# Two attentions on one core: Q and K by halves in two units, and a new order around the first unit's exponentials

## The chip, the cores and the metric

The kernel runs on one core of a Trainium2 chip. The metric is device time in microseconds (us), from the first to the last instruction with the little that lies around it; lower is better.

## What is computed

Two attention layers, independent of each other, with inputs of 2048 positions by 1024 features, 32 heads of 32 features, all in float32. Layer A is dilated: each position attends to 8 positions, two apart. Layer B is a sliding window of 256 positions. Both project the input to Q, K and V, and project the result with `wo`.

```python
qkv = (x @ wqkv).reshape(B, S, 3, H, Dh).transpose(2, 0, 3, 1, 4)
# layer A: W, dil = 8, 2; idx = pos[:, None] - arange(W) * dil, masked where negative
logits = einsum("bhsd,bhswd->bhsw", q, kg) * Dh ** -0.5
o = einsum("bhsw,bhswd->bhsd", softmax(logits), vg)
# layer B: mask = (i - j >= 0) & (i - j < 256)
scores = einsum("bhqd,bhkd->bhqk", q, k) * Dh ** -0.5
o = einsum("bhqk,bhkd->bhqd", softmax(where(mask, scores, -1e9)), v)
# both
return o.transpose(0, 2, 1, 3).reshape(B, S, D) @ wo
```

## The kernel before

**Units and head groups.** The work is cut into eight units of 512 positions: units 0 to 3 are layer B, units 4 to 7 layer A. In the code `u` is the unit, `DU` is 4 (the units of layer B), `U` is 8, and `s` counts the eight head groups (`NG`) of four heads in a unit; `hg = u * NG + s` numbers them through. Layer A's second and third unit are thus units 5 and 6, layer B's first is unit 0. All matmuls are done in three terms on values that are split in a high and a low part, so each x group and each weight is split after loading: a cast on ScalarE or VectorE (L276 or L279), then a subtraction on VectorE (L282). Loads go through three `raw` buffers; a buffer is loaded again when its split is done.

**Projections.** For each head group, Q and K are one accumulation each over eight blocks (`NK`) of three matmuls, the k-th block reading the k-th eighth of x and of the weights. x comes in four groups of two eighths. The list of items to load has, in units 5 and 6, Q's weights, x groups 0 and 1, K's weights, x groups 2 and 3. At the end of the unit before, the last part of V (narrow: two banks, sixteen blocks) is mixed with four items that ask for the next unit's x groups, one every four blocks from the second place on; asking writes the group's split into the engines' order.

**PSUM.** Three banks (`rg`) serve projections, four (`rs`) scores, one (`ro`) the values' results. Each ring gives out its banks in turn. A bank can be taken again when the copy that empties it is done: for V `copy_out` (L720 when on ScalarE), for Q and K `evac` (L625 in layer B, L586 and L591 in layer A).

**Attention of layer B.** `first` makes 16 score tiles for a head group. For each, `top` on VectorE (L1398) masks and takes the maximum, `total` on ScalarE (L1403) takes exponentials and their sum, which frees the score bank. When all 16 are done, `log_sum` and `parts` make the logarithm of the sums, `rows` puts it with a small matmul against the identity into rows, and `spread` (L1438) writes these into Q's stacked tile. Then `second` makes the scores anew, transposed, with the sums taken off; their exponentials (L1483) are masked, and `values` multiplies them with V. Q and K reach their stacked tiles by copies that SP issues, for units with a predecessor the last 256 keys of the unit before as well (`read_halo`). Layer A's scores work on small tiles (`window`).

**The order.** A planner in the Python code sets the order of every engine's instructions. It keeps a clock per engine with fixed costs, and four lists: row transpositions, second scores and values, first scores, and projections. At each step it takes the item that can start first by these clocks. Work that follows on other engines is written into their order when its time comes in the plan (`ck.defer(t, f)`: not before `t`). On the chip each engine runs its instructions in the order so written, waiting for semaphores. `done["stack"]` is the time from which the plan takes a head group's keys as there: the last copy's landing and `KEYS_LATE`, 1.2 us; `aux` holds the row transpositions.

Of the kernel before, what the change touches and what calls it, by code (L numbers as in the profile page):

```python
# [15 lines left out]
NG = 8  # L16
NK = 8
# [274 lines left out]
def kernel(ctx, tc, xs, wqk, wv, wo, outs, units):  # L292
# [271 lines left out]
    def latest(*ts):  # L564
        return None if any(t is None for t in ts) else max(ts)


    def qk_items(u, s):
# [8 lines left out]
        def read_halo():  # L577
            hb = halo[(u + 1) % 2][s]
            for r, a in enumerate((0, 1, 0)):
                nc.sync.dma_start(kst[buf][r:96:3, :, :256].bitcast(F32), hb[:, a])  # L580
                ck.copy("halo_in", ck.now)

        def evac_window(t, ps, bank):
            if t == 0:
# [35 lines left out]
        def evac(t, ps, bank):  # L620
            if not dense:
                return evac_window(t, ps, bank)
            hl = natp.tile([P, 2 * S + 16], F32R, tag="nat", name="nat")[:, :2 * S].rearrange("p (a s) -> p a s", a=2)
            sc = SCALE if t == 0 else 1.0
            nc.scalar.activation(hl[:, 0, :], ps, AF.Copy, scale=sc)  # L625
            r = ck.use("act", 0.485, ck.now + ck.SEM)

            def low():
                nc.vector.scalar_tensor_tensor(hl[:, 1, :], ps, sc, hl[:, 0, :].bitcast(F32), op0=ALU.mult,
                                               op1=ALU.subtract)  # L630
                e = ck.use("dve", 0.61, r)
                rg.give(bank, e)

                def stack():
                    e2 = place(1, e)
                    if t == 1:
                        done["stack"][u, s] = max(e2, h2["hi"]) + KEYS_LATE
                    if t == 1 and u + 1 < U and units[u + 1][3]:
                        nc.sync.dma_start(halo[u % 2][s], hl[:, :, 256:].bitcast(F32))
                        e2 = ck.copy("halo_out", e, ck.now)  # L640
                    done["nat"][2 * hg + t] = max(e2, h2["hi"])

                later(stack)

            def place(part, e):
                dst, c = (qst[buf], 0) if t == 0 else (kst[buf], 256)
                for i, a in enumerate((0, 0, 1) if t == 0 else (0, 1, 0)):
                    if a == part:
                        nc.sync.dma_start(dst[i:96:3, :, c:c + S].bitcast(F32), hl[:, a, :].bitcast(F32))
                        e2 = ck.copy("copy", e, ck.now)  # L650
                return e2

            def stack_hi():
                if t == 0 and has_halo:
                    read_halo()
                h2["hi"] = place(0, r)

            def later(f):
                if hg < 2 or hg - 2 in done["second"]:
                    f()  # L660
                else:
                    waiting.setdefault(hg - 2, []).append(f)

            later(stack_hi)
            ck.defer(r, low)
# [704 lines left out]
    def attention(u, s):  # L1370
# [11 lines left out]
        def first(b, j):  # L1382
            if "nm" not in h:
                h["nm"] = small.tile([P, 16], F32, tag="nm", name="nm")
                h["sm"] = small.tile([P, 16], F32, tag="sm", name="sm")
            full, mask = 384, cst["mask_d"]
            cut = 0 if has_halo else max(0, 256 - P * b)
            n = full - cut
            c1 = 256 + P * b + P
            c0 = c1 - n  # L1390
            i = j * 4 + b
            ps, bank = rs.take()
            mm(ps[:, :n], q[0:96, j, b * P:(b + 1) * P], kk[0:96, j, c0:c1],
                             start=True, stop=True)
            nm, sm = h["nm"][:, i:i + 1], h["sm"][:, i:i + 1]

            def top():
                nc.vector.tensor_tensor_reduce(ps[:, :n], ps[:, :n], mask[:, cut:full], scale=-1.0, scalar=BIG,  # L1398
                                               op0=ALU.add, op1=ALU.min, accum_out=nm)
                e = ck.use("dve", n / 960 + 0.114, ck.now) + 0.06  # L1400

                def total():
                    nc.scalar.activation(ps[:, :n], ps[:, :n], AF.Exp, bias=nm, scale=-1.0, accum_out=sm)  # L1403
                    e2 = ck.use("act", n / 1200 + 0.236, e)
                    rs.give(bank, e2)
                    h["left"] -= 1
                    if h["left"] == 0:
                        ck.defer(e2, log_sum)

                ck.defer(e - 0.1, total)  # L1410

            return top

        def log_sum():
            ln = small.tile([P, 16], F32, tag="ln", name="ln")
            nc.scalar.activation(ln, h["sm"], AF.Ln)
            e = ck.use("act", 0.13, ck.now) - 0.03

            def parts():
                nl = small.tile([P, 16], F32, tag="nl", name="nl")  # L1420
                nc.vector.tensor_tensor(nl, h["nm"], ln, op=ALU.subtract)
                hl = small.tile([P, 2, 16], F32R, tag="hl", name="hl")
                nc.vector.tensor_copy(hl[:, 0, :], nl)
                nc.vector.tensor_tensor(hl[:, 1, :], nl, hl[:, 0, :].bitcast(F32), op=ALU.subtract)
                e2 = ck.use("dve", 0.52, e, port=True)
                aux.append(Item(lambda: latest(rs.when(BANK_LATE), e2), lambda: rows(hl), 0.08))

            ck.defer(e, parts)

        def rows(hl):  # L1430
            ps, bank = rs.take()
            mm(ps[0:32, 0:P], hl.rearrange("p a b -> p (a b)"), cst["ident"], start=True, stop=True)

            def spread():

                h["rows"] = []
                for j in range(4):
                    nc.vector.tensor_tensor(q[96:P, j, :].rearrange("p (b s) -> p b s", s=P),  # L1438
                                            ps[0:32, None, 0:P].to_broadcast([32, 4, P]),
                                            cst["pick"][0:32, 4 * j:4 * j + 4, None].to_broadcast([32, 4, P]), op=ALU.mult)  # L1440
                    e = ck.use("dve", 0.61, ck.now)
                    h["rows"].append(e + ROWS_LATE)
                rs.give(bank, e)

            return spread
# [124 lines left out]
    for p in plan:  # L1570
        if not marks and p[1:] == (DU, 2) and p[0] == "qk":
            marks.append(len(gemm))
        if len(marks) == 1 and p[0] == "p":
            marks.append(len(gemm))
        if p[0] == "qk":
            new = qk_items(p[1], p[2])
            if p == ("qk", 0, 0):
                q, k, x = new[:NK], new[NK:], x_items(0)
                f = dict(FILL)
                new = x[0] + sum([q[i:i + 1] + fill(i + 1, f.get(i + 1, 0)) for i in range(4)], [])  # L1580
                for i in (1, 2, 3):
                    new[new.index(q[2 * i]) if i < 2 else len(new):0] = x[i]
                    if i == 1:
                        new += k[:4]
                    else:
                        new += q[2 * i:2 * i + 2] + k[2 * i:2 * i + 2]
            if p[1:] == (0, NG - 1):
                x1 = x1 or x_items(1)
                for g in range(3, FIRST_X - 1, -1):
                    new[NK + 2 * g - 2:NK + 2 * g - 2] = x1[g]  # L1590
            gemm += new
        elif p[0] == "v":
            new = v_items(p[1], p[2])
            if p[1:] == (0, 2) and FIRST_X:
                x1 = x_items(1)
                for g in range(FIRST_X - 1, -1, -1):
                    new[X1_AT[g]:X1_AT[g]] = x1[g]
            elif V_SLOTS.get(NG - 1) == p[2] and 0 < p[1] < U - 1:
                m = 2 * VPARTS[p[2]][1]
                for g, x in reversed(list(enumerate(x_items(p[1] + 1)))):  # L1600
                    new[m * g + XAT:m * g + XAT] = x
            gemm += new
        elif p[0] == "o":
            gemm += o_items(p[1], p[2])
        elif p[0] == "p":
            gemm += product(p[1], p[2])
        elif p[0] == "vp":
            new = value_product(p[2])
            if VP_AT.get((p[1], NG - 1)) == p[2:] and p[1] + 1 < U:
                for g, x in reversed(list(enumerate(x_items(p[1] + 1)))):  # L1610
                    new[4 * g + XAT:4 * g + XAT] = x
            gemm += new
# [87 lines left out]
```

## Time and profile before

| what | value |
|---|---|
| median of 3 runs | 1789.3 us (1788.56 to 1789.42) |
| the profiled execution | 1788.09 us, span 1786.4 us |
| TensorE (PE) busy | 1768.4 us, 99% of the span |
| VectorE (DVE) busy | 1295.5 us, 73% |
| ScalarE (ACT) busy | 936.9 us, 52% |
| GpSimd (POOL) busy | 412.8 us, 23% |
| HBM | 201.33 MB read, 53.48 MB written |

A row of the timeline has the start in us, the duration, the engine, the line, the operation, its tiles as out<-in, shapes and the count of instructions merged in it; in brackets the engine's idle time before it and what ended it. The stages' rows have, for each stretch, its length and each engine's busy time. Tile `g` is a projection's bank, `s` a score bank, `o` the values' bank; with `g`, the tile named first after the arrow is the one that streams.

### The profile page before, as it was taken

What the parts mean: (1) busy time and instruction counts of PE and PEld (TensorE: products, weight loads), DVE (VectorE), ACT (ScalarE), POOL (GpSimd) and SP (SyncE); (2) the same over time, 40 slices, a digit from 0 to 9 for tenths busy, and PEclk for the clock granted to TensorE, in tenths of its full rate; (3) what the DMA queues carried; (4) which work ended last, traced back from release to release, by engine and by line L of the source; (5) the groups of instructions that cost most, each with busy time, mean ns of one, the idle gap of its engine ahead of it and who ended that gap; (6) DMA issues with size and microseconds to landing.
All of it is one profiled execution on the core that took longest, in us unless ns stands there. A gap on an engine that the chain in (4) does not pass through costs nothing.

```text
span 1786.4 us, 38443 instructions
## 1 busy us (share of the span) xinstructions
PE 1768.4 (99%) x14496; PEld 1440.2 (81%) x14496; DVE 1295.5 (73%) x2881; ACT 936.9 (52%) x2332; POOL 412.8 (23%) x962
## 2 busy tenths in 40 slices
PE   9999999999999999999999999999999999999999
PEld 7787778888777888778788788878888887877887
DVE  6777876768867769867669546566577868767866
ACT  5565566555656565655654524444354546455442
POOL 3322324222333233242323410110011101001210
PEclk9999999999999999999999999999999999999999
DMA  8354664645645556555556255656576758948984
GB/s 256 106 151 136 187 167 137 163 135 152 186 142 154 154 127 173 150 148 156 133 142 186 72 181 180 210 193 209 175 219 197 233 169 290 303 151 271 310 319 144
DMA packets 154793, 324.57 MB, mean 182 GB/s; under 512 B 18032, under 2 KB 58992, under 8 KB 154608
## 3 DMA queue, kind: packets, MB, share of 16 engines
q0 software_dynamic: 45792, 166.74, 30.3%
q1 hardware_dynamic: 98736, 137.02, 26.9%
q10 hardware_dynamic: 10080, 18.35, 2.8%
q8 instruction: 115, 1.88, 0.4%
q14 instruction: 70, 0.57, 0.1%
HBM read 201.33 MB, written 53.48 MB: 143 GB/s over the span
## 4 chain that ended last, share of the span: by engine, by line
PE 92%; DVE 2%; DMA 2%; ACT 2%; issue 1%; SPq 0%; ACTq 0%; DVEq 0%; POOLq 0%
PE g L324 72%; PE s L324 13%; PE o L324 7%; DMA raw<-xs 1%; DVE w L282 1%; ACT s L1403 0%; DMA raw<-sd 0%; DMA pbuf<-nat 0%; DMA raw<-wqk 0%; DVE x L282 0%; ACT w L276 0%; DMA raw<-sx 0%; DMA qst<-nat 0%; ACT wide L1263 0%; ACT x L276 0%
## 5 line engine op out<-in xcount | busy, mean ns | idle before, releaser
L324 PE MATMUL g<-x,w 128*128 128x512 f32 x3552 | 875.8, 393 | 2.9 <-ACT x L276 1.0
L324 PEld LDWEIGHTS g<-x,w 128*128 128x128 f32 x3552 | 655.9, 188 | 131.7 <-issue 6.6
L282 DVE TENSOR_TENSOR w<-raw,w 128x512 fp32r<-128x512 f32 x510 | 334.3, 697 | 53.5 <-ACT w L276 47.2
L1398 DVE CUSTOM_DVE_ANT_0 s<-s,mask_d 128x384 f32<-128x384 f32 (+2 forms) x512 | 261.8, 554 | 98.4 <-PE s L324 98.1
L1403 ACT ACTIVATE s<-s,nm 128x384 f32<-128x384 f32 (+2 forms) x512 | 274.3, 537 | 109.9 <-DVE nm L1398 103.3
L324 PE MATMUL g<-w,x 128*128 128x256 f32 (+1 forms) x1728 | 306.9, 327 | 0.9 <-DVE w L282 0.7
L1462 POOL TENSOR_SCALAR_AFFINE_SELECT pbuf<-pbuf 128x128 f32<-128x128 f32 (+1 forms) x605 | 220.1, 392 | 315.7 <-ACT pbuf L1483 313.6
L324 PEld LDWEIGHTS g<-w,x 128*128 128x128 f32 x1728 | 255.3, 190 | 26.3 <-DVE w L282 2.2
L324 PE MATMUL g<-r,w 128*128 128x512 f32 x960 | 238.4, 393 | 0.5 <-DVE r L1362 0.5
L1483 ACT ACTIVATE pbuf<-s 128x384 f32<-128x384 f32 (+2 forms) x480 | 203.4, 504 | 65.3 <-PE s L324 63.5
L324 PEld LDWEIGHTS g<-r,w 128*128 128x128 f32 x960 | 177.2, 188 | 36.0 <-DVE r L1362 1.1
L221 POOL DMA_DIRECT2D raw<-wqk x126 | 68.4, 543 | 388.9 <-DVE w L282 265.2
L324 PEld LDWEIGHTS s<-qst,kst 128*128 128x128 f32 x704 | 113.5, 188 | 42.2 <-ACT s L1403 16.9
L324 PE MATMUL s<-kst,qst 96*128 96x384 f32 (+2 forms) x512 | 142.2, 342 | 0.9 <-ACT s L1403 0.7
L324 PE MATMUL s<-qst,kst 128*128 128x256 f32 (+2 forms) x704 | 137.0, 301 | 4.0 <-ACT s L1403 3.2
L279 DVE CAST w<-raw 128x1024 fp32r<-128x1024 f32 x176 | 121.3, 689 | 8.8 <-PE g L324 7.9
L324 PEld LDWEIGHTS s<-kst,qst 96*128 96x128 f32 x512 | 93.6, 189 | 26.2 <-issue 4.5
L276 ACT CAST w<-raw 128x1024 fp32r<-128x1024 f32 (+1 forms) x80 | 82.4, 1037 | 51.7 <-PE g L324 16.0
L1403 ACT ACTIVATION_READ_ACCUMULATOR s<-s,nm 128x1 f32 x512 | 105.3, 206 | 0.0
L1263 ACT COPY wide<-band 32x512 f32<-32x512 f32 x128 | 79.0, 617 | 30.3 <-DVE band L1254 28.8
L324 PE MATMUL o<-pbuf,vbuf 128*32 128x384 f32 (+2 forms) x1408 | 91.1, 388 | 0.0
L625 ACT ACTIVATE nat<-g 128x512 fp32r<-128x512 f32 x64 | 38.3, 598 | 97.7 <-PE g L324 87.1
(90 smaller groups left out, 1426.6 us busy)
## 6 DMA issues: line engine op xcount, KB each, us to landing
raw<-wqk POOLq DMA_DIRECT2D x126, 512.0 KB, 4.6
raw<-wv POOLq DMA_DIRECT2D x60, 512.0 KB, 4.8
qst<-nat SPq DMA_DIRECT2D x96, 256.0 KB, 4.2
kst<-nat SPq DMA_DIRECT2D x96, 256.0 KB, 5.5
raw<-wo POOLq DMA_DIRECT2D x44, 512.0 KB, 4.4
raw<-xs POOLq DMA_DIRECT2D x28, 512.0 KB, 4.5
kst<-halo SPq DMA_DIRECT2D x72, 128.0 KB, 4.5
pbuf<-nat SPq DMA_DIRECT2D x128, 65.0 KB, 3.2
```

The costliest lines, as they stand in the source:

```text
L221: (self.nc.scalar if early else self.nc.gpsimd).dma_start(raw if len(ap.shape) == 2 else raw.rearrange("p (a b) -> p a b", a=2), ap)
L276: nc.scalar.copy(t[:, 0, :], raw)
L279: nc.vector.tensor_copy(t[:, 0, :], raw)
L282: nc.vector.tensor_tensor(t[:, 1, c:c + 512], raw[:, c:c + 512], t[:, 0, c:c + 512].bitcast(F32), op=ALU.subtract)
L324: nc.tensor.matmul(out, left, right, **k)
L625: nc.scalar.activation(hl[:, 0, :], ps, AF.Copy, scale=sc)
L1263: nc.scalar.copy(diag[r:r + 32, :, :, c:c + 32], turned[r:r + 32, :, :, 1, :])
L1398: nc.vector.tensor_tensor_reduce(ps[:, :n], ps[:, :n], mask[:, cut:full], scale=-1.0, scalar=BIG, op0=ALU.add, op1=ALU.min, accum_out=nm)
L1403: nc.scalar.activation(ps[:, :n], ps[:, :n], AF.Exp, bias=nm, scale=-1.0, accum_out=sm)
L1462: nc.gpsimd.affine_select(w, w, pattern=[[0, m], [step, n]], compare_op=ALU.is_ge, fill=0.0, base=base, channel_multiplier=chan)
L1483: nc.scalar.activation(w, ps[:, :pack * n].rearrange("p (j n) -> p j n", j=pack), AF.Exp)
```

## The change

In units 5 and 6, the first head group's sixteen blocks are put in the order Q 0 to 3, K 0 to 3, Q 4 to 7, K 4 to 7. In unit 0, `total` is put into ScalarE's order from 0.7 us instead of 0.1 us before the plan has the maximum ready, and the row transposition is taken as ready 0.4 us later. For the last head group of unit 0 and the first of unit 1, the keys are taken as there 2.5 us later; and no head group's keys are taken as there before the last halo copy has landed.

```diff
@@ read_halo
-                ck.copy("halo_in", ck.now)
+                h2["halo"] = ck.copy("halo_in", ck.now)
@@ evac, stack
-                        done["stack"][u, s] = max(e2, h2["hi"]) + KEYS_LATE
+                        done["stack"][u, s] = max(max(e2, h2["hi"]) + (KEYS_LATE + 2.5 if hg in (NG - 1, NG) else KEYS_LATE), h2.get("halo", 0.0))
@@ first, top
-                ck.defer(e - 0.1, total)
+                ck.defer(e - (0.1 if u else 0.7), total)
@@ log_sum, parts
-                aux.append(Item(lambda: latest(rs.when(BANK_LATE), e2), lambda: rows(hl), 0.08))
+                aux.append(Item(lambda: latest(rs.when(BANK_LATE), e2 + (0.0 if u else 0.4)), lambda: rows(hl), 0.08))
@@ the list of projections
+            if DU < p[1] < U - 1 and p[2] == 0:
+                new = [new[c + i] for h in (0, NK // 2) for c in (0, NK) for i in range(h, h + NK // 2)]
```

## The prediction

> **What bounds the kernel now.** I read the page's head and its chain first, then the busy time by stages, then the stretches where TensorE rests, engine by engine.
>
> ```profile
> PE 1768.4 (99%) x14496; PEld 1440.2 (81%) x14496; DVE 1295.5 (73%) x2881; ACT 936.9 (52%) x2332; POOL 412.8 (23%) x962
> ...
> PE 92%; DVE 2%; DMA 2%; ACT 2%; issue 1%; SPq 0%; ACTq 0%; DVEq 0%; POOLq 0%
> ```
>
> TensorE is busy for 1768.4 of a span of 1786.4 us and carries 92% of the chain. The change removes no matmul, so all it can win is rest: 18.0 us, or a little more, since a busy TensorE is not TensorE at its peak. The rest near the edits:
>
> ```profile
> core 0: us, PE busy (x) PEld busy (x) DVE busy (x) ACT busy (x) POOL busy (x), PEclk, DMA share, GB/s
> ...
> 25.00:50.00 25.00, 25.00 (x117) 20.25 (x116) 16.80 (x54) 12.36 (x43) 2.54 (x4) 1.00 0.76 211
> 50.00:75.00 25.00, 24.38 (x135) 18.35 (x134) 19.73 (x54) 14.24 (x42) 7.35 (x20) 1.00 0.38 100
> ...
> 150.00:217.00 67.00, 64.04 (x378) 50.12 (x377) 56.37 (x154) 34.53 (x111) 21.16 (x45) 1.00 0.62 171
> ...
> 225.00:250.00 25.00, 25.00 (x145) 19.72 (x142) 19.83 (x53) 16.20 (x48) 6.91 (x19) 1.00 0.57 153
> ...
> 441.00:466.00 25.00, 24.03 (x154) 18.32 (x153) 22.93 (x59) 14.09 (x39) 7.01 (x14) 1.00 0.70 203
> ```
>
> Unit 0 fills roughly the first 240 us. After the start it rests in two places: 0.62 us in 50 to 75, and 2.96 us (67.00 less 64.04) in 150 to 217, where its last head groups meet unit 1's first. VectorE is busy 84% there (56.37 of 67.00), so its results come late.
>
> **Part 1: Q and K by halves, unit 5.** First group of layer A's second unit: sixteen blocks of three matmuls, Q's eight, then K's eight.
>
> ```profile
> 1143.75 4.27 PE L324 MATMUL g<-x,w 128*128 128x512 f32 x18
> 1148.97 0.50 PE L324 MATMUL g<-x,w 128*128 128x512 f32 x1 [0.95 <-ACT x L276]
> 1149.97 6.90 PE L324 MATMUL g<-x,w 128*128 128x512 f32 x29 [0.51 <-DVE x L282]
> 1156.71 0.62 PE L324 MATMUL g<-w,x 128*128 128x512 f32 x2
> ...
> 1321.09 11.07 PE L324 MATMUL g<-x,w 128*128 128x512 f32 x48
> 1331.99 1.30 PE L324 MATMUL g<-w,x 128*128 128x512 f32 x5
> ```
>
> In unit 6 (the last two rows) the 48 matmuls run from 1321.09 to 1331.99: 10.90 us, 0.227 each, with no wait. In unit 5 they take 12.96 us: 2.06 us are lost, at the seventh and eighth block of Q, which wait for the last x group. Only 0.95 and 0.51 of it show as rest, so a stretch loses 2.06/1.46 = 1.41 times the rest shown; I use this factor below.
>
> The new order asks for that x group later, after twelve matmuls each of Q and K. But K's first block now comes after twelve matmuls, and it needs a PSUM bank. There are three for projections: the narrow V part just before holds two and Q takes the third, so K gets the bank of V's first copy. In before K starts 24 matmuls after Q and the copy is long done. Where the copies stand on ScalarE:
>
> ```profile
> 1144.47 1.14 ACT L276 CAST x<-raw 128x512 fp32r<-128x512 f32 x2
> 1148.30 1.14 ACT L276 CAST x<-raw 128x512 fp32r<-128x512 f32 x2 [2.68 <-DMA raw<-xs]
> 1149.34 1.06 ACT L720 COPY vbuf<-g 128x512 f32<-128x512 f32 x2
> ...
> 1322.98 1.14 ACT L276 CAST x<-raw 128x512 fp32r<-128x512 f32 x2 [2.57 <-DMA raw<-xs]
> 1324.02 1.06 ACT L720 COPY vbuf<-g 128x512 f32<-128x512 f32 x2
> ```
>
> In both units the V copies (L720) stand behind the casts of the last x group, which wait for its load; the matmuls had finished by 1143.75 and 1321.09. The code asks for that group inside the V part, before the copies, and the change leaves that alone. So in unit 5 Q's first twelve matmuls end at 1143.75 + 2.72 = 1146.47, K's first waits for the first copy, 1149.34 + 0.53 = 1149.87, and with 0.1 for the hand-over the other 36 (8.17 us) end at 1158.1 instead of 1156.71: **+1.4 us**. The 2.06 us wait becomes one of 3.5 us. In unit 6 they would end at 1324.02 + 0.53 + 0.1 + 8.17 = 1332.8 instead of 1331.99: **+0.8 us**, where nothing was lost before. Both rest on a bank that has no row of its own; the other bound is that the copies come first (other engine, other order): then unit 5 wins its 2.06 and unit 6 stays, -2.1 us. I take the loss: nothing in the change moves the copy.
>
> ```profile
> PE g L324 <- DVE w L282: 0.5, 1, 0.5
> ```
>
> This wait is unit 5's next one (1143 to 1164), for V weights. If their split doesn't move with TensorE, a later TensorE finds them ready: that absorbs between 0 and 0.5 × 1.41 = 0.7; I take 0.4. Two things move along. Q's evacuation comes 12 matmuls later (2.7 us), and with it Q's four row copies on SP, now that much nearer to K's:
>
> ```profile
> pbuf<-nat SPq DMA_DIRECT2D x128, 65.0 KB, 3.2
> ```
>
> At 3.2 us to landing they are still in time, since the scores that read them wait for K's copies, which follow; if SP served them late it would cost at most these 3.2 us of a score date that lies a whole head group away, so I take 0. And the next V weights' split, asked for at K's third block, now stands ahead of Q's evacuation; it waits for its load on VectorE, Q's evacuation runs on ScalarE: 0. Part 1: **+1.8 us**, from -2.1 to +2.4.
>
> **Part 2: unit 0's exponentials 0.6 us forward.** ScalarE runs in the order written. An exponential (L1403) is now put into that order up to 0.6 us sooner, ahead of copies and casts that used to come first.
>
> ```profile
> 137.65 0.60 ACT L625 ACTIVATE nat<-g 128x512 fp32r<-128x512 f32 x1 [2.52 <-PE g L324]
> 138.15 0.34 ACT L1403 ACTIVATE s<-s,nm 128x128 f32<-128x128 f32 x1
> ...
> 166.22 0.41 DVE L1398 CUSTOM_DVE_ANT_0 s<-s,mask_d 128x256 f32<-128x256 f32 x1
> 166.41 1.30 ACT L720 COPY vbuf<-g 128x512 f32<-128x512 f32 x2 [4.02 <-PE g L324]
> 167.61 0.46 ACT L1403 ACTIVATE s<-s,nm 128x256 f32<-128x256 f32 x1
> 168.23 1.84 PE L324 MATMUL s<-qst,kst 128*128 128x384 f32 x4 [0.97 <-ACT s L1403]
> ...
> 206.32 0.58 ACT L1358 CAST r<-o 128x512 fp32r<-128x512 f32 x1
> 206.81 0.56 ACT L1403 ACTIVATE s<-s,nm 128x384 f32<-128x384 f32 x1
> 207.54 0.45 PE L324 MATMUL s<-kst,qst 96*128 96x384 f32 x1 [0.73 <-ACT s L1403]
> ```
>
> Three places show what the edit aims at. At 137.65 an evacuation that waits 2.52 us for TensorE holds up four exponentials. At 166.4 two V copies precede an exponential whose maximum was ready at about 166.8, so its score bank comes 0.8 us later than it could, and TensorE rests 0.97 us for it. At 206.3 a cast of 0.49 us (206.32 to 206.81) stands before the exponential for which TensorE rests 0.73. The most to win is the rest of both stretches with the factor: (0.62 + 2.96) × 1.41 = 5.0 us. It won't be all: part of it waits for VectorE (splits, rows), which the edit leaves as loaded as it is. The other way, an exponential set ahead of its own maximum holds ScalarE idle for up to 0.6 us, and the splits behind it get later; as bound I take the stretch's rest once more, +3.0 us. I take half of the gain, since three of these waits name L1403 and the rest do not: **-2.5 us**.
>
> **Part 3: later score rows and later keys.** In unit 0 the small transposition of the row sums is placed 0.4 us later; keys of unit 0's last and unit 1's first head group are taken as 2.5 us later, so other matmuls go first. Neither adds a semaphore; both only re-order TensorE. The halo term cannot bind: the halo copies are issued on SP ahead of the keys.
>
> ```profile
> PE s L324 <- ACT s L1403: 0.6, 1, 0.6
> ...
> 213.56 0.45 PE L324 MATMUL s<-kst,qst 96*128 96x128 f32 x3
> 213.85 2.30 PE L324 MATMUL g<-w,x 128*128 128x512 f32 x9
> 216.50 0.41 PE L324 MATMUL s<-qst,kst 128*128 128x384 f32 x1 [0.36 <-DVE qst L1438]
> ...
> 239.19 0.52 PE L324 MATMUL s<-kst,qst 96*128 96x384 f32 x2
> 239.55 1.55 PE L324 MATMUL g<-x,w 128*128 128x512 f32 x6
> ```
>
> The first row is the only wait of 50 to 52: the row transposition waits 0.6 us for its bank, and one block of 0.68 us ahead of it would cover that. At 213.56 and 239.19 the two head groups' scores start without a wait, so the keys were there: the later date saves nothing there and moves 3 and 2 score matmuls behind projections. Three score banks come free at 213.56, which may help the 0.36 wait at 216.50. These gains lie in the 5.0 us already counted; I add **-0.1**, from -0.5 to +1.4 (0.97, the rest of 441 to 466, × 1.41: one more unit crossing that waits, if the later group is missed at unit 1's end).
>
> **Sum:** +1.8 - 2.5 - 0.1 = -0.8 us on this execution's own time, 1788.1 us (1.7 us around the span), so 1787.3. The median of the runs shown is 1.2 us above the profiled one, so I forecast **1788.5 us**. About 0.2% (3.6 us) is what I hold a measurement of this kernel able to tell from none: the bounds are 1785.7 and 1792.9.
>
> **The rivals.**
>
> *Halves work as written (0.17).* If the V copies get ahead of the x casts, part 1 gives -2.1: -4.7 in all, 1784.6. For it: the load order already has K's weights between the x halves. Against: ten casts and copies in two units, all in the order shown.
>
> *ScalarE waits for maxima (0.08, the other side).* Exponentials ahead of their maxima block evacuations and weight casts in unit 0. Part 2 turns to +3.0: 1.8 + 3.0 - 0.1 = +4.7, 1794.0. Unit 0 has 8 × 16 exponentials; five full 0.6 us holds on TensorE's path cancel part 2's gain, and ten decide it. For it: VectorE at 84% in 150 to 217. Against: three projection banks, so an evacuation has a block's time to spare.
>
> *The long wait slows TensorE (0.05).* 3.5 us in unit 5 would be by far its longest rest.
>
> ```profile
> 1.52 4.03 PE L324 MATMUL s<-qst 128*128 128x512 f32 x10 [1.52 <-DVE qst L1616]
> ```
>
> After the idle start ten matmuls took 4.03 us, 0.40 each instead of 0.227. The same again would cost 10 × 0.18 = 1.8 us: +1.0, 1790.3. Against it, the granted clock reads 1.00 in every stretch quoted. The Trainium skill ("TensorE: Matmul & The Clock Gate", Part 1) says that TensorE falls to half clock after an idle window of about 3.4 us and needs as long to recover. By that rule a wait of 3.5 us is just long enough if it fills a window; the slow start agrees, the clock column doesn't show it.
>
> *Another rhythm in units 1 to 3 (0.10).* The order is planned anew after every shift.
>
> ```profile
> 457.41 1.81 ACT s L1403 x6
> ...
> 713.45 1.82 ACT s L1403 x6
> ```
>
> The same step of the chain returns 256.04 us later, so the plan settles into one pattern, and what changes it counts three times: 3 × 0.97 × 1.41 = 4.1 us if that crossing wait vanishes or doubles. 1784.4 or 1792.6.
>
> **How the numbers follow.** The forecast has 0.60, with 1786 to 1791 as its own range: part 2 between -5.0 and 0 around it. Below 1785.7 lie two thirds of the halves rival (0.11), half of the rhythm (0.05), and the forecast's tail where unit 0 gives all (0.06): 0.22. Above 1792.9: the ScalarE rival (0.06), rhythm and tail (0.04): 0.10. Within: 0.68. The range 1783.3 to 1792.6 leaves out about a tenth below and above together, its ends near the rhythm's and the halves' times.
>
> **What would show it.** In unit 5, a rest of about 3.4 us after Q's twelfth matmul, released by ACT vbuf L720, and in unit 6 one of about 0.7. In 150 to 217, less waiting on ACT s L1403, rest down from 2.96 to 1 to 2 us. At 50 to 52 no wait. From about 350 us on the same rhythm, with the wait near 457. I am wrong if K's first block runs without a wait (then the copies moved), or if 150 to 217 rests 3 us or more.

## The result, and the profile after

The change makes the kernel slower by 0.2%: 1792.23 us median (1789.36 to 1794.57) against 1788.40 us for the kernel before, run beside it (1786.28 to 1791.97); ratio 1.0020, 95% interval 1.0014 to 1.0026. The forecast was 1788.5 us with a sum of -0.8 us. The range held the time, the sign was wrong. The profiled execution of the changed kernel took 1794.57 us (span 1792.9), the longest of its 21 runs; it is read here for places, and the ratios for sizes. One per mille of the time is 1.79 us.

First the page's head and chain after, then four of the stages that the prediction showed:

```profile
PE 1772.1 (99%) x14496; PEld 1442.5 (80%) x14496; DVE 1296.4 (72%) x2873; ACT 938.1 (52%) x2332; POOL 415.0 (23%) x970
...
PE 89%; DMA 4%; DVE 4%; ACT 1%; issue 1%; POOL 0%; SPq 0%; ACTq 0%; DVEq 0%; POOLq 0%
```

```profile
core 0: us, PE busy (x) PEld busy (x) DVE busy (x) ACT busy (x) POOL busy (x), PEclk, DMA share, GB/s
50.00:75.00 25.00, 24.82 (x137) 18.89 (x137) 17.78 (x47) 13.69 (x40) 7.97 (x23) 1.00 0.38 114
150.00:217.00 67.00, 64.78 (x386) 51.81 (x385) 59.34 (x155) 33.68 (x106) 25.99 (x48) 1.00 0.58 164
225.00:250.00 25.00, 24.10 (x127) 17.78 (x127) 20.96 (x54) 14.28 (x42) 6.81 (x16) 1.00 0.58 153
441.00:466.00 25.00, 24.03 (x152) 18.22 (x152) 22.96 (x59) 14.39 (x40) 7.38 (x14) 1.00 0.70 200
```

TensorE's matmuls are as many as before, and yet it is busy for 3.7 us longer (1772.1 against 1768.4): some of its matmuls have become slow, as rows below show. Its rest has grown too, from 18.0 to 20.8 us. Unit 0 is not where this comes from: the rest in 50 to 75 has gone from 0.62 to 0.18, in 150 to 217 from 2.96 to 2.22 (0.90 of rest is new in 225 to 250). Unit 1's crossing at 441 rests 0.97 us as before, and the two that follow (697 to 722 and 953 to 978) rest 1.27 and 0.61 us against 0.97 and 0.61, so the rhythm of units 1 to 3 is the old one.

Next, units 5 and 6: the timeline of TensorE and ScalarE.

```profile
1143.64 2.91 PE L324 MATMUL g<-x,w 128*128 128x512 f32 x12
1148.94 10.06 PE L324 MATMUL g<-x,w 128*128 128x512 f32 x36 [2.40 <-ACT vbuf L720]
1158.84 0.84 PE L324 MATMUL g<-w,x 128*128 128x512 f32 x3
...
1147.27 1.14 ACT L276 CAST x<-raw 128x512 fp32r<-128x512 f32 x2 [1.74 <-DMA raw<-xs]
1148.32 1.06 ACT L720 COPY vbuf<-g 128x512 f32<-128x512 f32 x2
...
1323.05 2.91 PE L324 MATMUL g<-x,w 128*128 128x512 f32 x12
1326.20 8.50 PE L324 MATMUL g<-x,w 128*128 128x512 f32 x36 [0.24 <-ACT vbuf L720]
1334.54 0.84 PE L324 MATMUL g<-w,x 128*128 128x512 f32 x3
```

K's first block does wait for the bank of V's first copy, right after Q's twelfth matmul, in both units. In unit 5 the wait is 2.40 us, and the 36 matmuls behind it take 10.06 us, where unit 6's 36 take 8.50. From the start of Q to the next block unit 5 now has 1158.84 - 1143.64 = 15.20 us against 12.96 before: +2.24. Unit 6 has 1334.54 - 1323.05 = 11.49 against 10.90: +0.59.

The largest loss is in unit 7, whose Q and K the change does not touch. TensorE's timeline at its start, before and then after:

```profile
1503.07 11.07 PE L324 MATMUL g<-x,w 128*128 128x512 f32 x48
1513.98 1.52 PE L324 MATMUL g<-w,x 128*128 128x512 f32 x6
1515.69 0.50 PE L324 MATMUL g<-w,x 128*128 128x512 f32 x1 [0.19 <-DVE w L279]
1516.42 0.73 PE L324 MATMUL g<-w,x 128*128 128x512 f32 x2 [0.22 <-DVE w L282]
1517.08 1.12 PE L324 MATMUL o<-wide,vbuf 128*32 128x136 f32 x32
1518.13 4.16 PE L324 MATMUL g<-w,x 128*128 128x512 f32 x17
```

```profile
1505.28 6.07 PE L324 MATMUL g<-x,w 128*128 128x512 f32 x26
1512.77 5.29 PE L324 MATMUL g<-x,w 128*128 128x512 f32 x22 [1.42 <-DVE w L282]
1517.89 1.52 PE L324 MATMUL g<-w,x 128*128 128x512 f32 x6
1520.83 0.50 PE L324 MATMUL g<-w,x 128*128 128x512 f32 x1 [1.42 <-DVE w L279]
1521.56 0.87 PE L324 MATMUL g<-w,x 128*128 128x512 f32 x2 [0.23 <-DVE w L282]
1522.36 2.02 PE L324 MATMUL o<-wide,vbuf 128*32 128x136 f32 x32
1524.30 1.92 PE L324 MATMUL g<-w,x 128*128 128x512 f32 x5
```

From Q's start to the projection behind the values there are 1524.30 - 1505.28 = 19.02 us against 1518.13 - 1503.07 = 15.06: +3.96. Two waits for split weights have become long (behind the second matmul of K's first block, 1.42 us where there was none; at the projection after K, 1.42 us where there was 0.19), and the 32 matmuls of the values took 2.02 us instead of 1.12. The first wait is the one to follow: the second is 1.0 us long in two kernels below that are not slower than before, and so is no sign of this loss.

The slow matmuls have their own view. Cut at the times at which the granted clock changes in this trace, the stretches read:

```profile
1146.51:1149.93 3.42, 1.02 (x5) 0.85 (x5) 3.32 (x8) 2.11 (x4) 1.08 (x2) 1.00 0.66 200
1149.93:1153.34 3.41, 3.41 (x9) 2.64 (x9) 2.84 (x4) 2.73 (x5) 0.74 (x2) 0.50 0.97 287
1153.34:1156.75 3.41, 3.41 (x16) 2.80 (x15) 0.00 (x0) 2.40 (x6) 0.70 (x1) 1.00 0.79 263
...
1518.57:1521.98 3.41, 1.77 (x7) 0.86 (x5) 3.31 (x6) 3.24 (x8) 0.53 (x1) 1.00 1.06 353
1521.98:1525.40 3.42, 3.42 (x37) 2.29 (x36) 3.32 (x6) 1.12 (x3) 0.53 (x1) 0.50 0.89 247
```

After a stretch of 3.41 us in which TensorE worked for 1.02 us, and after one with 1.77, it ran for the next 3.41 us at half clock: 9 matmuls fit in it where 16 do at full clock.

### The profile page after: what moved, and what is told of

Same layout as the page of the kernel before. It is cut to its first block, busy times and chain, and to the rows that moved or that the text cites. A ratio compares the mean times of both kernels' runs of the same rounds, so it can differ in the third digit from the quotient of the medians.

```text
span 1792.9 us, 38459 instructions
## 1 busy us (share of the span) xinstructions
PE 1772.1 (99%) x14496; PEld 1442.5 (80%) x14496; DVE 1296.4 (72%) x2873; ACT 938.1 (52%) x2332; POOL 415.0 (23%) x970
## 4 chain that ended last, share of the span: by engine, by line
PE 89%; DMA 4%; DVE 4%; ACT 1%; issue 1%; POOL 0%; SPq 0%; ACTq 0%; DVEq 0%; POOLq 0%
PE g L324 71%; PE s L324 12%; PE o L324 6%; DMA raw<-xs 2%; DVE w L282 1%; DMA raw<-wqk 1%; DMA raw<-tv 1%; ACT s L1403 0%; DMA qst<-nat 0%; DVE w L279 0%; DMA pbuf<-nat 0%; DVE s L1398 0%; DVE x L282 0%; DVE qst L1438 0%; ACT x L276 0%
```

## The experiments

All were timed in rounds beside the kernel before. Each ratio is to before, with its 95% interval; it is not the quotient of the two medians beside it, and sizes in per mille and in us below are worked out from it. The expectations call the wait for V's copy the bank theory; "the halves alone" is the first kernel below.

| kernel | median us (before beside it) | ratio |
|---|---|---|
| halves alone | 1793.28 (1787.72) | 1.0025 (1.0015 to 1.0034) |
| unit 0's edits alone | 1785.73 (1787.72) | 0.9987 (0.9978 to 0.9996) |
| halves in unit 5 alone | 1788.98 (1787.72) | 1.0004 (0.9995 to 1.0013) |
| halves, last x groups later | 1789.18 (1787.72) | 1.0005 (0.9996 to 1.0014) |
| unit 6's new order alone | 1789.25 (1788.08) | 1.0012 (1.0003 to 1.0021) |
| halves, unit 6's old order | 1789.67 (1788.08) | 1.0011 (1.0002 to 1.0020) |
| halves, wait filled | 1792.77 (1788.08) | 1.0030 (1.0019 to 1.0042) |
| Q then K, K's weights behind x | 1787.40 (1788.08) | 0.9999 (0.9990 to 1.0007) |
| exponentials alone | 1785.99 (1788.75) | 0.9988 (0.9979 to 0.9997) |
| later keys alone | 1789.32 (1788.75) | 1.0004 (0.9995 to 1.0013) |
| unit 0's edits, K's weights behind x | 1785.80 (1788.75) | 0.9986 (0.9977 to 0.9995) |
| the whole change, unit 6's old order | 1788.53 (1788.75) | 1.0001 (0.9992 to 1.0010) |

**The two halves of the change.** First the projections' edit alone, then all the other edits without it.

```diff
 # halves alone: before, and
+            if DU < p[1] < U - 1 and p[2] == 0:
+                new = [new[c + i] for h in (0, NK // 2) for c in (0, NK) for i in range(h, h + NK // 2)]
 # unit 0's edits alone: after, without these two lines
```

> The kernel before with the halves alone. Its order differs from before's from unit 6's layer A scores on, as the changed kernel's does, and nowhere in unit 0. Bank theory (K's first block waits for the V copies that stand behind the last x casts on ScalarE): TensorE waits about 2.4 us for ACT vbuf L720 in unit 5, which costs 2.2 us net there, and 0.5 us net in unit 6, so +2.5 to +4.5 us with what follows in unit 7. Unit 0 theory (the exponentials' edit costs the time): within 1 us of before.

> The changed kernel without the halves: only the edits of unit 0 and of the keys. Bank theory: between -1.0 and 0 us, since the changed kernel's trace stands 0.4 us ahead at 360 us and its order is before's again from there on. Unit 0 theory: +2 us or more.

The halves alone lose 2.5 per mille, 4.5 us; unit 0's edits win 1.3 per mille, 2.3 us. The two add up to the change within the intervals. So the whole loss is the halves', and unit 0's edits win about what the prediction gave them, more than the 1.0 us at most that was expected ahead of this run.

**Unit 5 alone, and the copies first.** Halves in unit 5 only leave layer A's order in unit 6 as it was. The other kernel asks for the last two x groups inside the halves, ahead of K's first and third block, so that V's copies come first on ScalarE.

```diff
 # halves in unit 5 alone
-            if DU < p[1] < U - 1 and p[2] == 0:
+            if p[1] == DU + 1 and p[2] == 0:
 # halves, last x groups later
+                for at, x in zip((4, 6), held_x[p[1]]):
+                    new[at:at] = x
```

> Halves in unit 5 alone; every other instruction of TensorE is in before's order, unit 7's too. Bank theory: +2.2 us, all of it between 1143 and 1165, and nothing after. Unit 7 theory (the loss is the new order of layer A's scores in unit 6 and the later loads of unit 7): at most +1 us.

> Halves in units 5 and 6, but the last two x groups are asked for inside the halves (ahead of K's first and third block), not in the V part before, so the V copies come first on ScalarE. Bank theory: no wait for ACT vbuf L720, and the 2.06 us of x waits in unit 5 go as well: 2 us ahead of before at 1165, 4 us ahead of the halves alone; the order of 1324 to 1599 is new, worth 2 us either way. If the bank is not what K waits for: the same +2 to +3 us at 1165 as the halves alone.

With unit 5 alone the wait for V's copy is there (2.24 us in its trace) and unit 7's waits are not; the loss is 0.4 per mille (-0.5 to 1.3), not told apart from none. With the last x groups later the wait for the copy is gone, as the waits of 1143 to 1164 show:

```profile
PE g L324 <- DVE w L279: 0.7, 1, 0.7
PE g L324 <- DVE w L282: 0.5, 1, 0.5
```

So the bank is what K waits for in the change. Unit 5 wins less than the 2 us expected, 0.84 us in this trace (from the start of Q to the block behind K 1155.67 - 1143.55 = 12.12 us against 12.96), since K's first block now waits 0.7 us for K's weights. The time did not fall below before's: this kernel's order in units 6 and 7 is another one again, and its trace gives back there what unit 5 won, in part in a slow stretch at 1498.55.

**Order or lateness.** The halves change the plan: from unit 6 on, 27 of 207 picks of the planner fall differently, and layer A's scores and values stand a few projections sooner or later. Here the picks are forced, once the new ones on the kernel before, and once the old ones on the halves and on the whole change.

```diff
+    forced, start = "g12ggg...", 2573
...
+        at = sum(pos.values()) - start
+        if 0 <= at < len(forced):
+            t = seqs[forced[at]][pos[forced[at]]].ready()
+            best = None if t is None else (max(t, ck.now), forced[at])
```

> The kernel before, Q then K as it was, but layer A's score and value steps in unit 6 are put between the projections at the places where the halves put them (27 picks of 207 differ, all before unit 7). Theory (order): the 4.3 us lost in unit 7 come from this order, through ScalarE: the cast of a weight tile now stands behind the copy of an attention output and holds up the ring of raw buffers. Then unit 5 and unit 6 stay as before, unit 7 loses 2.5 to 4.5 us, time 1790 to 1792. Rival (lateness): unit 7 loses because TensorE comes 2.7 us late out of units 5 and 6, and the order is harmless. Then the time stays at before's within 0.8 us.

> Both units by halves, but layer A's score and value steps in unit 6 stay at the places that they have before. Theory (order): the waits in units 5 and 6 stay (+0.5 to +2.2 and +0.6 us), unit 7's loss goes: 1 to 3 us above before, 2.5 to 4.5 below the halves alone (1793.3). Rival (lateness): as slow as the halves alone, within 1 us.

> The whole change, but layer A's score and value steps in unit 6 stay at the places that they have before (27 picks of 207). Theory (order): the loss in unit 7 goes, the waits in units 5 and 6 and the gain of unit 0 stay: 1787 to 1788.5, 3.5 to 5 below the change as it is (1792.2), no slower than before. Rival (lateness): as slow as the change within 1 us.

The new order alone, with no halves at all, brings unit 7's two waits (TensorE's timeline of that kernel):

```profile
1502.95 6.09 PE L324 MATMUL g<-x,w 128*128 128x512 f32 x26
1510.42 5.28 PE L324 MATMUL g<-x,w 128*128 128x512 f32 x22 [1.39 <-DVE w L282]
...
1518.21 0.50 PE L324 MATMUL g<-w,x 128*128 128x512 f32 x1 [1.15 <-DVE w L279]
```

It costs 1.2 per mille, 2.1 us (0.5 to 3.8): less than the 2.5 to 4.5 us that the order theory expected, but outside the rival's 0.8 us only by the middle of its interval. Its one trace does not show that size: from the start of unit 5's Q to that of unit 7's it is 1.42 us faster than before (1502.95 - 1145.05 against 1503.07 - 1143.75), from there to the last matmul 1.66 us slower, and most of what this execution lost, 1.30 us, it had lost ahead of unit 5, where its order is before's. So the trace gives the place and the timings the size. The other two decide it. The halves in the old order lose 1.1 per mille where the halves lose 2.5, and the parts add up: 1.1 + 1.2 = 2.3. The whole change in the old order is level with before (1.0001), 1.9 per mille or 3.4 us below the change as it is, and the two intervals do not meet. So what the halves lose beyond their own 1.1 per mille is the order's.

TensorE's lateness is not what brings unit 7's first wait. With the halves in the old order it says little, as TensorE is 0.7 us behind before at 1488 but only 0.10 at unit 7's Q. But with the halves in unit 5 alone, in before's order, TensorE comes to unit 7's Q 2.75 us later than before (1.63 of it from ahead of unit 5), and nothing there waits; with the new order alone it comes 0.12 us sooner, and waits 1.39. These are the halves in unit 5 alone, and the whole change in the old order:

```profile
1505.82 11.05 PE L324 MATMUL g<-x,w 128*128 128x512 f32 x48
1516.71 2.64 PE L324 MATMUL g<-w,x 128*128 128x512 f32 x9
```

```profile
1501.22 11.07 PE L324 MATMUL g<-x,w 128*128 128x512 f32 x48
...
1514.65 0.49 PE L324 MATMUL g<-w,x 128*128 128x512 f32 x1 [1.00 <-DVE w L279]
```

The wait inside Q and K is in the traces of all four kernels that have the halves' order in unit 6 (0.69 to 1.42 us) and in none of the other traces. The second wait is in some of both: it is 1.00 us here and 1.02 with unit 0's edits alone. The last trace loses time later in unit 7 all the same, in a wait of 1.3 us for row copies (DMA pbuf<-nat) and a slow stretch at 1552.44, so that the old order costs nothing is read off its 11 runs and not off this one.

How the order reaches unit 7 is read off VectorE's timeline, before and with the new order alone.

```profile
1490.69 1.79 DVE L1104 TENSOR_TENSOR r<-r 128x256 f32<-128x256 f32 x4
...
1500.53 1.28 DVE L282 TENSOR_TENSOR x<-raw,x 128x512 fp32r<-128x512 f32 x2
...
1507.21 1.28 DVE L282 TENSOR_TENSOR w<-raw,w 128x512 fp32r<-128x512 f32 x2
```

```profile
1498.88 1.29 DVE L282 TENSOR_TENSOR x<-raw,x 128x512 fp32r<-128x512 f32 x2 [0.81 <-ACT x L276]
...
1501.29 1.79 DVE L1104 TENSOR_TENSOR r<-r 128x256 f32<-128x256 f32 x4
1503.00 1.29 DVE L282 TENSOR_TENSOR x<-raw,x 128x512 fp32r<-128x512 f32 x2
...
1509.68 1.28 DVE L282 TENSOR_TENSOR w<-raw,w 128x512 fp32r<-128x512 f32 x2
...
1505.37 1.05 ACT L276 CAST w<-raw 128x1024 fp32r<-128x1024 f32 x1 [2.81 <-DMA raw<-wqk]
```

A side task, the sum of tiles of another weight (L1104, in `half_sums`), has moved. Before it is done at 1490.69, ahead of unit 7's x splits; with the new order it stands among them, at 1501.29, and the third x split comes at 1503.00 instead of 1500.53: 2.47 us later, 1.71 of it by this task. The other 0.76 is there from unit 7's first x group on and fits a chain of loads: on ScalarE a weight's cast stands behind the copy of an attention result, which waits for TensorE, and comes at 1478.24 instead of 1476.44; the load after it is asked for at 1481.13 instead of 1479.35, and the first x group's at 1487.24 instead of 1486.21.

From 1498.88 on VectorE works without a rest, and K's low part, for which TensorE waits until 1510.42, starts at 1509.68 instead of 1507.21, the same 2.47 us late. The cast of K's weights on ScalarE is late as well (1505.37 against 1504.35), but it ends 3.26 us before VectorE comes to the low part, so it is not what TensorE waits for. The task stands at 1489 to 1494 in the seven traces with before's order in unit 6, and at 1501 to 1504, between two x splits, in the four with the halves' order. That it carries the loss is argued from these rows; no run moved it by itself.

**The clock.** Nine more matmuls were put into unit 5's wait (they add to Q's own bank, so that head group gets another Q), and in another kernel, with Q then K, all x groups were loaded ahead of K's weights, which shortens the wait that before has there.

```diff
 # halves, wait filled
+                if (u, s, t, k) == (DU + 1, 0, 0, 3):
+                    for i in range(9):
+                        nc.tensor.matmul(h["ps"], h["w"][:, 0, k * P:(k + 1) * P], xt[u][k][:, 0, :], start=False, stop=False)
 # Q then K, K's weights behind x
-                    unit_x(p[1], 0, 1)
+                    unit_x(p[1], 0, 1, 2, 3)
                     item(("qk", p[1], 0, 1), "w", wqk[units[p[1]][0], 1])
-                    unit_x(p[1], 2, 3)
```

> The halves alone, with nine more matmuls of Q's fourth block in unit 5 (2.04 us, into Q's own bank; layer A's second unit gets another Q for its first head group by it), so that TensorE works through most of the wait for V's first copy. No order changes. Theory (clock): the wait of 2.1 to 2.4 us lets the granted clock fall to half for one window of 3.41 us behind it, which costs up to 1.7 us. With the wait filled the clock stays at 1.00 in 1149 to 1156, the 36 matmuls behind it take 8.2 to 8.4 us and not 9.9, and the time is 0.8 to 1.7 us below the halves alone, the drop not falling into every run. Rival (contention): the 36 matmuls are slow for another reason (casts and copies on the same memory beside them), and stay at 9.9 us; the time is that of the halves alone, or above it where the nine matmuls outlast the wait.

> The kernel before, Q then K as it was; the loads of units 5 and 6 are asked for in another order: all four x groups, then K's weights (before: two x groups, K's weights, two x groups). Theory (bank and order): the wait of Q's seventh and eighth block in unit 5 (2.06 us) goes or shrinks below 0.7, unit 5 wins 1.4 to 2 us; layer A's order in unit 6 differs here too, so up to 4 us can be lost in unit 7 again: 1786 to 1790. Rival (the load is the limit): K's weights then come too late by what x came sooner, and unit 5 wins nothing: 1787.5 to 1792.

In the filled kernel's trace the 36 matmuls take 8.46 us at a granted clock of 1.00, as the clock theory expected:

```profile
1146.32 2.20 PE L692 MATMUL g<-x,w 128*128 128x512 f32 x9
1149.06 8.46 PE L324 MATMUL g<-x,w 128*128 128x512 f32 x36 [0.53 <-ACT vbuf L723]
```

But a kernel that fills nothing shows the same. These are the halves alone, and the halves with unit 6's old order:

```profile
1148.85 10.07 PE L324 MATMUL g<-x,w 128*128 128x512 f32 x36 [2.15 <-ACT vbuf L720]
```

```profile
1148.48 8.45 PE L324 MATMUL g<-x,w 128*128 128x512 f32 x36 [2.27 <-ACT vbuf L720]
```

The same stretch, with the longer wait in the fast one: a wait of this length is sometimes followed by the slow clock and sometimes not. So one profile proves nothing for the fill, and its time (3.0 per mille over before) is no lower than that of the halves alone: the gain that the theory expected in the median is not there. The load order of the last kernel takes unit 5's wait down to 0.47 us in its trace, and none of its 11 runs is below a granted clock of 1.000, where 50 of 94 runs of before, beside these experiments, are. It wins no time that can be told from none.

**Which edit of unit 0.** Exponentials alone, and later keys alone.

```diff
 # exponentials alone
-                ck.defer(e - 0.1, total)
+                ck.defer(e - (0.1 if u else 0.7), total)
 # later keys alone
-                        done["stack"][u, s] = max(e2, h2["hi"]) + KEYS_LATE
+                        done["stack"][u, s] = max(e2, h2["hi"]) + (KEYS_LATE + 2.5 if hg in (NG - 1, NG) else KEYS_LATE)
```

> The kernel before with unit 0's exponentials 0.6 us forward in ScalarE's order, nothing else of the change. Theory (exponentials): the whole of unit 0's gain (2.0 us) is theirs, as the prediction had it: 1785.5 to 1786.5, where before is near 1788. Rival (keys): the gain comes from the later keys, this kernel stays at before's time within 0.8 us.

> The kernel before with the keys of unit 0's last and unit 1's first head group taken as 2.5 us later, nothing else of the change. Theory (exponentials): no gain, within 0.5 us of before. Rival (keys): 1.5 to 2 us faster.

The exponentials win 1.2 per mille, 2.1 us, as much as all of unit 0's edits; the later keys by themselves can't be told from no change.

**A version that beats both.** Unit 0's edits without the halves, with the load order above (the diff is the two put together).

> Unit 0's edits together with the load order of units 5 and 6 in which all x groups come ahead of K's weights; Q then K, no halves. Theory (the two add up): the 2.0 us of unit 0 and the 0.7 us of the load order, and no run at a lower granted clock, since unit 5's long wait is gone: 1785.0 to 1785.6, closer together than before's runs. Rival (the load order is worth nothing, its clock an accident): the time and the spread of unit 0's edits alone, near 1785.8 to 1786.2, one run in five above 1788.

It is 1.4 per mille faster than before. The load order adds nothing to unit 0's edits alone that could be measured, and 2 of its 11 runs are below a clock of 1.000, so the expectation that none would be fell. Unit 0's edits without the halves are what is worth keeping.

## Why the prediction was wrong

**What failed** is a step that the prediction did not make: it followed part 1 through units 5 and 6 and stopped there. It knew that the order is planned anew after every shift, but priced that only as a rhythm of units 1 to 3. Halves that delay and reorder 16 blocks in unit 6 shift layer A's scores and values there, a side task on VectorE moves in front of unit 7's splits, and K's low part comes late. Part 1 was summed at +1.8 us, +2.4 at most (its own terms without the absorbed 0.4 add to +2.2); it measures +4.5 (2.7 to 6.1). Of it, the halves in the old order are +2.0 (0.4 to 3.6), near the +1.8; the order is +2.1 (0.5 to 3.8), which had no term. That the range held the time all the same is luck. Neither of the two signs of being wrong that the prediction named has come: K's first block waits, and 150 to 217 rests less than 3 us.

**Part 1's own steps.** The bank of V's first copy is what K waits for, behind the last x casts on ScalarE: right in both units. Unit 5's wait was put at 3.4 us and is 2.40, since the casts stand at 1147.27 instead of 1148.30: the load came sooner than in the profile of before. In the halves with the old order, at full clock, unit 5's sixteen blocks lose some 0.5 us (Q starts at 1143.30 there and the block behind K at 1156.78: 13.48 against 12.96), not the +1.4; at half clock they lose 2.24. Unit 6: +0.8 forecast, +0.59 measured in the change. So the +2.0 agrees with the +1.8 better than its terms do. The 0.4 that V's weights were to absorb was not absorbed: their wait is 0.5 us as before.

**Part 2** was right: -2.5 forecast, -2.1 measured (-3.8 to -0.5). TensorE's waits for these exponentials in 100 to 240, 2.1 us before, are down to 0.9 with unit 0's edits alone, and with the exponentials alone to this:

```profile
PE s L324 <- ACT s L1403: 0.4, 1, 0.4
```

The rest in 150 to 217 is a poorer measure: 1.09 us in the trace of unit 0's edits alone, inside the 1 to 2 forecast, but 2.22 in that of the whole change and 2.73 with the exponentials alone, where other waits have come in (1.0 us for split weights in the change, 1.6 us for a copy of keys with the exponentials alone). At 50 to 52 a wait of 0.18 us is left where none was forecast.

**Part 3** (-0.1) is not contradicted: later keys alone +0.7 us (-0.9 to +2.3). The later score rows were not timed alone.

**The rivals.** The halves do not work as written, ScalarE does not wait for maxima, and the rhythm of units 1 to 3 is unchanged. The slow clock was given 0.05 on the ground that it needs a wait of about 3.4 us; it came behind one of 2.40. In the profiled execution it costs about 10.06 - 8.45 = 1.6 us in unit 5 and, by its second stretch (half of 3.42 us), up to 1.7 in unit 7. Yet it doesn't explain the result. A stretch of 3.41 us at half clock takes 0.5 x 3.41 / 1790 = 0.00095 off a run's mean clock, so runs at 1.000 have had none. Of 21 runs of the change, 8 are at 1.000, with a median of 1790.9 us, 9 at 0.999 with 1792.6 and 4 at 0.998 with 1794.0. Of before's 94 runs beside the experiments, 44 are at 1.000 with 1787.5, 38 at 0.999 with 1788.8 and 12 at 0.998 with 1790.0. The change loses 3.4 us among runs that had no slow stretch, so the clock makes part of the spread within a kernel and little of the difference between the two.

## What to carry to other kernels

Where a planner writes the order, price an edit past its own place: compare the planned order of all engines to the end, and look where a side task has moved in front of a split that TensorE needs, because here the unedited unit behind the edit lost as much as the edited ones. When two edits are made at once, time each alone: here one won 2.3 us and the other lost 4.5, and the sum hid both. Look at the granted clock of every run before explaining a difference of a microsecond or two by one profile.

## What the runs showed of the hardware

The granted clock changes in stretches of 3.41 us on a grid that runs through the whole execution. In the change the two slow stretches begin at 1149.93 and 1521.98, in the halves alone at 1150.30 and 1522.35:

```profile
1146.89:1150.30 3.41, 1.45 (x6) 1.23 (x7) 3.31 (x8) 2.11 (x4) 0.95 (x2) 1.00 0.68 197
1150.30:1153.71 3.41, 3.41 (x9) 2.64 (x9) 2.72 (x4) 2.84 (x5) 0.86 (x2) 0.50 1.00 299
1518.94:1522.35 3.41, 1.64 (x6) 0.67 (x4) 3.31 (x7) 3.24 (x8) 0.53 (x1) 1.00 1.06 338
1522.35:1525.77 3.42, 3.42 (x36) 2.47 (x36) 3.32 (x6) 1.17 (x4) 0.53 (x1) 0.50 0.99 270
```

Both pairs are 372.05 us apart, which is 109.0 times 3.413; in three more traces the two slow stretches start 84.0, 69.0 and 474.0 times that apart. TensorE had worked for 1.02 to 1.77 us of the 3.41 ahead of each. So the length of a wait does not decide it alone, but also how much of it falls into one stretch of the grid, and the grid lies elsewhere in every run. That would explain why the wait of 2.15 us was followed by slow matmuls and the one of 2.27 us was not: the grid of that trace, counted back from its slow stretch at 1785.92, behind the last matmul, has an edge at 1147.62, in the middle of the wait, and TensorE is busy for 2.00 and 2.56 us of the stretches on either side. Busy time is not the whole of it. In unit 0 a stretch with 2.31 us of work was followed by half clock in two traces (halves in unit 5 alone, unit 6's new order alone) and by full clock in a third (the halves alone). Where the limit lies, and what it counts, is open. The Trainium skill ("TensorE: Matmul & The Clock Gate", Part 1) has the clock fall to half after an idle window of about 3.4 us, in windows that run freely. The traces agree on the windows' length, on the half and on their running freely. They differ on the idle window: here one with TensorE 30% to 52% busy was enough.
